# Score maxima of sliding-window attention in 9 products of 128 by 128 instead of 18 of 64 by 96, on one Trainium2 core

## The chip, the core and the metric

The kernel runs on one core of a Trainium2 chip. The metric is the device time of one launch in microseconds. Engines: PE multiplies matrices (PEld loads its weights), DVE and ACT work on vectors, POOL copies between SBUF tiles and issues the loads, SP issues the stores. Work of different engines is ordered by semaphores; each engine takes its own instructions in order.

## What is computed

Sliding-window causal attention over 8 batches of 8 heads, 576 positions, 64 channels, followed by a soft mixture of experts with 32 slots and 8 experts.

```python
scores = (q @ k.T) / 8                        # per batch and head, 576 x 576
mask = (i - j >= 0) & (i - j < 64)
scores = where(mask, scores, -1e9)
attn = exp(scores - scores.max(-1)); attn /= attn.sum(-1)
x = (attn @ v) laid out as 4608 x 512
logits = x @ phi                              # 4608 x 32
d = softmax of logits over the 4608 rows;  c = softmax over the 32 slots
slot = d.T @ x                                # 32 x 512, four slots for each expert
out = c @ (relu(slot[e] @ w1[e]) @ w2[e])     # w1: 8 x 512 x 1024, w2: 8 x 1024 x 512
```

All inputs are float32 in HBM and are turned into float16 by the DMAs that load them; the output, 9.4 MB, is float32.

## The kernel before

**Stages.** A loop of 32 stages works on pairs of heads, four pairs to a batch. The order on every engine is the order in which the program writes the work down; stage n runs several pairs at once, each at another step:

- `join(n+1)` (L108, POOL): two copies, of k and q, that bring a pair's rows together;
- `turn` (L259, PE) turns k and q of pair n; `keep_k` (L269) and `keep_q` (L266), on ACT, write `kT` and `qz`;
- `score_main(n-3)` (L320, L323, PE): for 8 blocks a product that adds mask and minus the row maximum (`lh` by `rt`), then the scores; `keep_main` (L328, ACT) takes their exponential into `pt`; `score_last` (L311, L312) and `keep_last` (L316, ACT) do the ninth block;
- `st_turn(n-5)`: `turn_x` (L363, PE) and `keep_x` (L370, DVE) turn the finished x;
- `st_mask` (L274, L275) and `st_max(n-1)` (L291, PE): masks and scores of pair n-1 once more, with queries on the partitions, into `mx`; `keep_max` (L296, DVE) takes the row maxima into `m`;
- `st_av(n-4)` (L340, PE) multiplies `pt` with the values; `st_norm` (L349, L350, DVE) divides;
- `st_shift(n-2)` (L300, PE) turns the maxima, `keep_shift` (L303, DVE) writes them into `rt`, where `score_main` finds them a stage later.

From stage 8 on each stage also has a quarter of the routing of a batch (`fi` in the code, here the letters A to D). A (`fi` 0): logits, copied by `keep_logits` (L384), and their maxima `nb`, `run` (L388, L389, DVE). B (`fi` 1): exponentials `dd` and `al` (L395, L396, ACT). C (`fi` 2): `turn_dispatch` (PE), `keep_dispatch` (L420, ACT, into `dT`), slot sums `si`, added up by `keep_slots` (L469, DVE). D (`fi` 3): an exponential (L431, ACT) and a transposition (L438, DVE).

**PSUM.** `kb`, `tx`, `qb` and `lg` or `si` share a ring of two banks; `sc`, `av` and `mx` have two banks each. `score_last` and `st_shift` use spare columns of `av`.

**Scores for the maxima before.** A block of 32 queries of two heads sees at most 96 keys, so that 18 products of 64 columns by 96 keys do, two to each block of 64 queries, one on the upper and one on the lower half of the partitions:

```python
for i in range(9):
    for t in range(2):
        o = 64 * i + 32 * t
        nc.tensor.matmul(mx[64 * t:64 * t + 64, i // 5, 96 * (i % 5):96 * (i % 5) + 96],
                         heads(p, o, 32), kT[:, o:o + 96], start=False, stop=True, ...)
```

**Loads.** POOL issues every load, between its copies: q and k of two pairs (`load_qk`), half a batch of values (`load_v`, then copied by `shift_v`), and weights (`load_w`), one transfer in every fourth stage and one in every stage from 25 on. The last six transfers are halves of the last three experts' `w2`.

**Tail.** After the loop the last pairs are finished, the slots go through the experts (`first` L800, `turned`, `second` L823), and `cps` (L861, ACT L865, DVE L867, store L869) writes the output in 19 stores, first the left half of the columns of two groups, then their right half, then two groups whole.

Of the kernel before, what the change touches and what calls it, by code (L numbers as in the profile page):

```python
# [20 lines left out]
def kernel(  # L21
# [114 lines left out]
    for t_, src in reversed(tuple(zip(firsts, (q, k)))):  # L136
# [9 lines left out]
    lh = const.tile([128, 9, 128], FP16, name="lh")  # L146
    nc.vector.memset(lh, 0.0)
    warm = lh[:, 0:4, :].rearrange("p i x -> p (i x)")
    NQ = 4
    qzs = [pqk.tile([128, 2 * S], FP16, name=f"qz{i}") for i in range(NQ)]  # L150
    kTs = [pqk.tile([128, 64 + S], FP16, name=f"kT{i}") for i in range(NQ)]
    sides[0] = (pil.tile([GP, RQ, 2, Dh], FP16, name="qi", tag="qi"),
                pil.tile([GP, RQ, 2, Dh], FP16, name="ki", tag="ki"))
    KR = 74
    nc.scalar.activation(lh[64:KR], ident_h[64:KR, 64:KR - 1].unsqueeze(2).broadcast_to([KR - 64, 9, 128]),
                         AF.Copy, scale=-1.0)
    nc.vector.memset(qzs[0], 0.0)
    nc.vector.memset(kTs[0][:, 0:64], 0.0)
    for t_, src, eng in zip(sides[0], firsts, (nc.scalar.copy, nc.vector.tensor_copy)):
# [3 lines left out]
    wb = ctr[0:32, 0:96]  # L163
    nc.gpsimd.memset(wb, 0.0)
    nc.gpsimd.affine_select(out=wb, in_=wb, compare_op=ALU.is_gt, fill=NEG,
                            base=0, pattern=[[1, 96]], channel_multiplier=-1)
    nc.gpsimd.affine_select(out=wb, in_=wb, compare_op=ALU.is_ge, fill=NEG,
                            base=64, pattern=[[-1, 96]], channel_multiplier=1)
    mb = ctr[0:64, 96:224]
# [6 lines left out]
    NR = 2  # L176
    sel = const.tile([128, 4, 32], FP16, name="sel")
    wm = const.tile([128, 5, 96], FP16, name="wm")
    for t in (0, 64):
        nc.vector.tensor_copy(out=sel[t:t + 32],  # L180
                              in_=ident_h[t:t + 32, t:t + 32].unsqueeze(1).broadcast_to([32, 4, 32]))
        nc.vector.tensor_copy(out=sel[t + 32:t + 64].rearrange("p (t l) x -> p t (l x)", t=2),
                              in_=ident_h[t + 32:t + 64, t + 32:t + 34].unsqueeze(2).broadcast_to([32, 2, 64]))
        nc.vector.memset(wm[t + 32:t + 64], 0.0)
        nc.vector.tensor_copy(out=wm[t:t + 32], in_=wb.unsqueeze(1).broadcast_to([32, 5, 96]))
    nc.vector.memset(wm[32:33, 0, 0:64], NEG)
    nc.vector.memset(wm[32:34, 0, 0:32], NEG)
    av = pav.tile([128, 2, 512], FP32, name="av", tag="av")
    mx = pmx.tile([128, 2, 512], FP32, name="mx", tag="mx")
    nc.vector.memset(mx[:, 1, 384:480], 0.0)  # L190
    ms = [const.tile([128, 33], FP16, name=f"m{i}") for i in range(2)]
    for t_ in ms:
        nc.vector.memset(t_[:, 10:33], 0.0)
    for t_, z_ in zip(kTs[1:], qzs[1:]):
        nc.vector.memset(t_[:, 0:64], 0.0)
        nc.vector.memset(z_, 0.0)
    nc.vector.memset(av[64:128, :, 260:325], 1.0)
    rts = [const.tile([128, 128], FP16, name=f"rt{i}") for i in range(NR)]
    for rt in rts:
        nc.vector.memset(rt, 0.0)  # L200
    for i in range(3):
        nc.vector.memset(vrs[i][:, :, 64], 1.0)
    for i in range(2):
        nc.vector.memset(vss[i][:, :, 64], 1.0)
        nc.vector.memset(vss[i][0:64, 0, 0:64], 0.0)
    lgs = pf.tile([128, 192], FP32, name="lgs")
    nc.vector.memset(lgs[0:96, 128:192], -3.0e38)
    dd = pf.tile([128, 256], FP16, name="dd")
    nc.vector.memset(dd[:, 192:256], 0.0)
    run = pmo.tile([128, 3], FP32, name="run")  # L210
    stat, nmax = run[:, 0:1], [run[:, 1:2], run[:, 2:3]]
    nc.vector.memset(nmax[1], 1.0e30)
    nc.vector.memset(stat, 0.0)
# [6 lines left out]
    def constants(part):  # L220
        if part == 2:
            nc.vector.tensor_copy(out=lh[0:64], in_=mb[:, :].unsqueeze(1).broadcast_to([64, 9, 128]))
            for rt in rts:
                nc.vector.tensor_copy(out=rt[64:KR, :], in_=ident_h[64:KR, KR - 1:KR].broadcast_to([KR - 64, 128]))
                nc.vector.tensor_copy(out=rt[0:64, :].rearrange("p (t l x) -> p t l x", t=2, l=2),
                                      in_=ident_h[0:64, 0:64].rearrange("p (t x) -> p t x", t=2)
                                      .unsqueeze(2).broadcast_to([64, 2, 2, 32]))
            nc.vector.scalar_tensor_tensor(out=lh[64:KR, 0, 0:64],  # L228
                                           in0=ident_h[64:KR, KR - 1:KR].broadcast_to([KR - 64, 64]),
                                           scalar=NEG, in1=lh[64:KR, 0, 0:64], op0=ALU.mult, op1=ALU.add)  # L230
# [41 lines left out]
    def st_mask():  # L272
        st = sel.rearrange("p a x -> p (a x)")
        nc.tensor.matmul(mx[:, 0, 0:480], st[0:64], wm[0:64, 0:5, :], start=True, stop=False, skip_group_check=True)  # L274
        nc.tensor.matmul(mx[:, 1, 0:384].rearrange("p (c e x) -> p c e x", e=3, x=32)[:, :, 0::2, :],  # L275
                         st[64:128], wm[64:128, 1:5, :].rearrange("p c (e x) -> p c e x", e=3)[:, :, 0::2, :],
                         start=True, stop=False, skip_group_check=True)

    def heads(p, o, w):
        a = qzs[p % NQ][:, 2 * o:2 * o + 2 * w]  # L280
        return a if w == 32 else a.rearrange("p (t l x) -> p l t x", t=2, l=2)

    def turned_max(p):
        return rts[p % NR][:, :].rearrange("p (t l x) -> p l t x", t=2, l=2)

    def st_max(p):
        kT = kTs[p % NQ]
        for i in range(9):
            for t in range(2):
                o = 64 * i + 32 * t  # L290
                nc.tensor.matmul(mx[64 * t:64 * t + 64, i // 5, 96 * (i % 5):96 * (i % 5) + 96],  # L291
                                 heads(p, o, 32), kT[:, o:o + 96], start=False, stop=True,
                                 skip_group_check=True)

    def keep_max(p):
        nc.vector.reduce_max(ms[p % 2][:, 0:10].rearrange("p (h c) -> p h c", h=2),  # L296
                             mx[:, :, 0:480].rearrange("p h (c x) -> p h c x", x=96), axis=AXX)
# [4 lines left out]
    def keep_shift(p, to, eng=nc.vector.tensor_copy):  # L302
        eng(out=rts[p % NR][64:73, :], in_=to[0:9])  # L303
# [14 lines left out]
    def score_main(p, sc, u0=0, u1=2, o=0):  # L318
        for i in range(4 * u0, 4 * u1):
            nc.tensor.matmul(sc[:, i // 4 - o, 128 * (i % 4):128 * (i % 4) + 128], lh[:, i, :], turned_max(p),  # L320
                             start=(i % 4 == 0), stop=False, skip_group_check=True)
        for i in range(4 * u0, 4 * u1):
            nc.tensor.matmul(sc[:, i // 4 - o, 128 * (i % 4):128 * (i % 4) + 128],  # L323
                             kTs[p % NQ][:, 64 * i:64 * i + 128], heads(p, 64 * i, 64),
# [210 lines left out]
    for n in range(NP):  # L535
        b, hp = divmod(n, HP)
        if n + 1 < NP:
# [4 lines left out]
        elif n == 1:  # L542
            load_v(0, (1,))
            load_qk(3)
        elif n % 2 == 0 and n // 2 + 3 < 2 * B:
# [3 lines left out]
        constants(n)  # L549
# [16 lines left out]
        if n >= 3:  # L566
# [4 lines left out]
            score_last(n - 3, av[:, 0, 328:456])  # L571
            keep_last(n - 3, av[:, 0, 328:456])
# [6 lines left out]
        qb = bank([128, 1024], FP16, "qb")  # L579
        if fi == 2:  # L580
            turn_dispatch(qb[:, 640:800])
        turn(sides[n][0], qb)
        if fi == 2:
            keep_dispatch(fb, qb[:, 640:800])
        keep_q(n, qb)
        if n >= 1:
            st_mask()
        if n >= 4:
            st_av(n - 4, av)
        if n == NP - 3:  # L590
            to_row(nmax[O % 2], av[0:1, 0, 352:480])
        elif n == NP - 2:
            to_rows(rO, av[:, 0, 340:341])
        if n >= 2:
            st_shift(n - 2, av[64:97, 1, 384:512])
            keep_shift(n - 2, av[64:97, 1, 384:512])
        if n == NP - 3:
            row_min(rO, av[0:1, 0, 352:480])
            nc.gpsimd.tensor_scalar(out=pO, in0=nmax[O % 2], scalar1=-1.0, scalar2=None, op0=ALU.mult)
        elif n == NP - 2:  # L600
            nc.scalar.activation(fO, av[:, 0, 340:341], AF.Exp, bias=pO)
        if 4 <= n < NP - 1:
# [11 lines left out]
        if n >= 1:  # L614
            keep_max(n - 1)
        if fi == 0:
            keep_logits(lg, nc.vector.tensor_copy)
# [28 lines left out]
    R, W, X, Y = NP - 4, NP - 3, NP - 2, NP - 1  # L646
    kb = bank([128, 512], FP32, "kb")
# [260 lines left out]
```

## Time and profile before

| | us |
|---|---|
| three runs | 194.35, 195.71, 192.37 (median 194.35) |
| the profiled execution, its own time | 192.44 |
| its span in the profile | 190.7 |
| busy: PE, DVE, ACT, POOL | 155.2, 139.8, 129.3, 129.8 |
| mean granted clock of PE | 0.889 |
| read from HBM, written | 61.93 MB, 9.44 MB |

Busy time is the union of an engine's instructions. A row of the timeline gives the start, the time taken, the engine, the line, the operation, the tiles written and read, and in brackets the idle time before and what ended it. DMA shares count 16 engines as one; packets in flight together count twice, so that a share may be above 1.

### The profile page before, as it was taken

How to read it: one execution, taken by the hardware profiler on the slowest of the kernel's cores; microseconds unless marked ns; L12 is line 12 of the kernel's file. 1: busy time of each engine (PE TensorE's matmuls, PEld its weight loads, DVE VectorE, ACT ScalarE, POOL GpSimd, SP SyncE). 2: the span in 40 equal slices, each digit the busy share in tenths (PEclk: the TensorE clock that was granted, in tenths of full speed). 3: DMA queues.
4: the chain of work that ended last, by engine and by line, in shares of the span. 5: the costliest groups of instructions: out<-in, count | busy, mean ns of one | idle time of the engine just before them, and what ended most of it. 6: DMA issues, size and time to landing. Idle time of an engine off the chain costs nothing.

```text
span 190.7 us, 6941 instructions
## 1 busy us (share of the span) xinstructions
PE 155.2 (81%) x2897; PEld 116.2 (61%) x2897; DVE 139.8 (73%) x322; ACT 129.3 (68%) x244; POOL 129.8 (68%) x254
## 2 busy tenths in 40 slices
PE   1858888988898898988989779997888999999400
PEld 0538777867687677776868657676666446564000
DVE  4786688888799979978879987887775754689500
ACT  5672787879778797887977888787664052668400
POOL 8989999976979879888897877965988440000000
PEclk9975699999999999999999999999999699555555
DMA  6999999999999999999999999999999999999996
GB/s 149 148 184 184 201 199 184 173 224 177 184 220 183 183 221 180 185 223 178 182 215 188 188 217 211 198 213 213 217 218 199 198 198 180 249 342 342 399 415 269
DMA packets 64447, 41.14 MB, mean 216 GB/s; under 512 B 38816, under 2 KB 61856, under 8 KB 62880
## 3 DMA queue, kind: packets, MB, share of 16 engines
q0 software_dynamic: 58320, 30.68, 118.1%
q1 hardware_dynamic: 6096, 10.03, 14.6%
q8 instruction: 22, 0.36, 0.7%
q14 instruction: 9, 0.07, 0.1%
HBM read 61.93 MB, written 9.44 MB: 374 GB/s over the span
## 4 chain that ended last, share of the span: by engine, by line
PE 38%; DVE 32%; ACT 11%; issue 10%; POOL 2%; DVEq 0%; ACTq 0%; POOLq 0%
DVE m L296 9%; DVE x_b L350 8%; PE cp L861 7%; PE av L340 6%; ACT qz L266 3%; PE sc L320 3%; PE hh L800 3%; PE sc L323 3%; DVE rt L303 2%; PE ops L823 2%; ACT pt L328 2%; DVE rc L349 2%; PE mx L291 2%; PE qb L259 2%; ACT pt L316 2%
## 5 line engine op out<-in xcount | busy, mean ns | idle before, releaser
L266 ACT ACTIVATE qz<-qb 64x576 f16<-64x576 f16 x64 | 41.2, 643 | 1.8 <-PE qb L259 1.2
L296 DVE TENSOR_REDUCE m<-mx 128x10 f16<-128x960 f32 x32 | 36.8, 1149 | 0.6 <-PE mx L291 0.6
L328 ACT ACTIVATE pt<-sc 128x1024 f16<-128x1024 f32 x29 | 29.6, 1022 | 9.4 <-PE sc L323 8.7
L269 ACT ACTIVATE kT<-kb 128x576 f16<-128x576 f16 x32 | 20.8, 650 | 13.6 <-PE kb L259 13.2
L350 DVE TENSOR_TENSOR x_b<-av,rc 128x640 f16<-128x640 f32 x31 | 25.6, 824 | 1.1
L259 PE MATMUL qb<-ident_h,qi 96*128 96x96 f16 x192 | 14.2, 212 | 8.9 <-DVE acc L469 3.5
L303 DVE CAST rt<-av 9x128 f16<-9x128 f32 x30 | 8.7, 289 | 16.5 <-PE av L300 15.7
L117 POOL DMA_DIRECT2D vr<-in_v_dram x16 | 20.0, 1249 | 0.0
L323 PE MATMUL sc<-qz,kT 128*128 128x128 f16 x232 | 18.6, 223 | 0.7 <-issue 0.7
L320 PE MATMUL sc<-rt,lh 128*128 128x128 f16 x232 | 18.6, 225 | 0.6 <-DVE rt L303 0.6
L291 PE MATMUL mx<-kT,qz 128*64 128x96 f16 x576 | 18.7, 211 | 0.0
L340 PEld LDWEIGHTS <-pt 128*64 128x64 f16 x576 | 12.7, 110 | 9.3 <-ACT pt L316 4.4
L259 PEld LDWEIGHTS <-qi 96*128 96x128 f16 x192 | 11.5, 101 | 10.6 <-issue 9.5
L323 PEld LDWEIGHTS <-kT 128*128 128x128 f16 x256 | 16.5, 100 | 0.9 <-issue 0.9
L108 POOL COPY qi<-qs 96x384 int32<-96x384 int32 x31 | 15.6, 503 | 1.8 <-DMA qs<-in_q_dram 0.9
L320 PEld LDWEIGHTS <-lh 128*128 128x128 f16 x256 | 16.2, 100 | 0.7 <-DVE lh L228 0.4
L108 POOL COPY ki<-ks 96x384 int32<-96x384 int32 x31 | 15.6, 503 | 1.1
L865 ACT ACTIVATE ob<-cp,rcs 128x256 f32<-128x256 f32 (+1 forms) x27 | 13.2, 546 | 3.9 <-PE cp L861 3.6
L291 PEld LDWEIGHTS <-qz 128*64 128x64 f16 x576 | 15.6, 113 | 0.5 <-issue 0.4
L259 PE MATMUL kb<-ident_h,ki 96*128 96x96 f16 x192 | 14.6, 216 | 1.1 <-DVE xt L370 0.6
L340 PE MATMUL av<-vr,pt 128*64 128x65 f16 x279 | 15.4, 197 | 0.0
L340 PE MATMUL av<-vs,pt 128*64 128x65 f16 x279 | 13.7, 198 | 1.8 <-ACT pt L316 1.8
(198 smaller groups left out, 367.8 us busy)
## 6 DMA issues: line engine op xcount, KB each, us to landing
w<-in_moe_w_dram POOLq DMA_DIRECT2D x12, 1024.0 KB, 15.2
vr<-in_v_dram POOLq DMA_DIRECT2D x16, 288.0 KB, 11.8
out_dram<-ob SPq DMA_DIRECT2D x6, 768.0 KB, 7.0
ks<-in_k_dram POOLq DMA_DIRECT2D x15, 288.0 KB, 9.5
qs<-in_q_dram POOLq DMA_DIRECT2D x15, 288.0 KB, 10.3
out_dram<-ob SPq DMA_DIRECT2D x11, 384.0 KB, 4.3
w<-in_moe_w_dram POOLq DMA_DIRECT2D x8, 512.0 KB, 13.8
xt<-in_k_dram SPq DMA_DIRECT2D x1, 288.0 KB, 3.1
```

Of the source, the lines that this page charges most:

```text
L108: nc.gpsimd.tensor_copy(out=d_, in_=s_.rearrange("p h r d -> p r h d"))
L117: nc.gpsimd.dma_start(out=vrs[b % 3][:, c0:c1, 0:64], in_=src[:, c0:c1, :])
L259: nc.tensor.transpose(tp[:, j, :], src[:, j].rearrange("p h d -> p (h d)"), ident_h[0:GP, 0:GP])
L266: nc.scalar.activation(dst[r, hl], src[r], AF.Copy, scale=scale)
L269: nc.scalar.activation(kTs[p % NQ][:, 64:64 + S].rearrange("p (g j) -> p g j", j=RQ), ps[:, 0:RQ * GP].rearrange("p (j g) -> p g j", j=RQ) ...
L291: nc.tensor.matmul(mx[64 * t:64 * t + 64, i // 5, 96 * (i % 5):96 * (i % 5) + 96], heads(p, o, 32), kT[:, o:o + 96], start=False, stop=Tru ...
L296: nc.vector.reduce_max(ms[p % 2][:, 0:10].rearrange("p (h c) -> p h c", h=2), mx[:, :, 0:480].rearrange("p h (c x) -> p h c x", x=96), axi ...
L320: nc.tensor.matmul(sc[:, i // 4 - o, 128 * (i % 4):128 * (i % 4) + 128], lh[:, i, :], turned_max(p), start=(i % 4 == 0), stop=False, skip_ ...
L323: nc.tensor.matmul(sc[:, i // 4 - o, 128 * (i % 4):128 * (i % 4) + 128], kTs[p % NQ][:, 64 * i:64 * i + 128], heads(p, 64 * i, 64), start= ...
L328: nc.scalar.activation(pts[p][:, 0:8, :, :], sc[:, :, :].rearrange("p u (c l x) -> p (u c) l x", l=2, x=64), AF.Exp)
L340: nc.tensor.matmul(av[r0:r0 + 64, hl, 65 * (i // 2):65 * (i // 2) + 65], pt[:, i, hl, :], values(b, h, i), start=True, stop=True, skip_gro ...
L350: nc.vector.tensor_tensor(out=x_b[:, :, 128 * hp:128 * hp + 128].rearrange("p c (l d) -> p l c d", l=2), in0=avv[:, :, :, 0:64], in1=rc[:, ...
```

## The change

The scores for the maxima are made for 64 queries of two heads at a time, with 128 columns by 128 keys. Eight such products fill the two banks of `mx`, the ninth (`st_max_last`, `keep_max_last`, tile `m8`) goes to the columns of `av` that `score_last` had. The masks are no longer `sel` and `wm`; `st_mask` multiplies what `score_main` uses too (`lh`, `rt`), and a copy `low` for the lower half of the partitions. One row of `lh` falls away.

```diff
 def st_mask():
-    nc.tensor.matmul(mx[:, 0, 0:480], st[0:64], wm[0:64, 0:5, :], ...)
-    nc.tensor.matmul(mx[:, 1, 0:384] ..., st[64:128], wm[64:128, 1:5, :] ..., ...)
+    for r, u, keys in ((slice(0, 64), 0, lh[0:64, 0:4, :]), (slice(64, 128), 1, low[64:128, 1, :] x4)):
+        nc.tensor.matmul(mx[:, u, :], (low[r, 0, :] if u else rts[0][r, :]), keys, start=True, ...)
 def st_max(p):
-    for i in range(9): for t in range(2):  # 64 columns by 96 keys
+    for i in range(8):
+        nc.tensor.matmul(mx[:, i // 4, 128 * (i % 4):128 * (i % 4) + 128], queries(p, i),
+                         kTs[p % NQ][:, 64 * i:64 * i + 128], start=False, ...)
+def st_max_last(p, to):
+    nc.tensor.matmul(to, rts[0][0:64, :], lh[0:64, 8, :], start=True, stop=False, ...)
+    nc.tensor.matmul(to, queries(p, 8), kTs[p % NQ][:, 512:640], start=False, stop=True, ...)
 def keep_max(p):
-    nc.vector.reduce_max(ms[..][:, 0:10], mx[:, :, 0:480] by 96, axis=AXX)
+    nc.vector.reduce_max(ms[..][:, 0:8], mx by 128, axis=AXX)
+def keep_max_last(p, to):
+    nc.vector.reduce_max(ms[p % 2][:, 8:9], to, axis=AXX)
```

In the stage the order becomes this (`qz` has its heads in runs of 64 and no longer of 32):

```diff
             score_main(n - 3, sc); keep_main(n - 3, sc)
-            score_last(n - 3, av[:, 0, 328:456]); keep_last(n - 3, av[:, 0, 328:456])
 ...
         turn(sides[n][0], qb)
         if fi == 2: keep_dispatch(...)
-        keep_q(n, qb)
-        st_mask()
+        score_last(n - 3, s8)                   # s8: spare columns of qb
+        late = fi in (0, 2)
+        if not late: keep_q(n, qb); keep_last(n - 3, s8)
+        st_max_last(n - 1, m8)                  # m8: spare columns of av
         st_av(n - 4, av)
         st_shift(n - 2, ...)
-        keep_shift(n - 2, ...)                  # DVE
+        keep_shift(n - 2, ..., nc.scalar.copy if fi in (0, 2) else nc.vector.tensor_copy)
+        if late: keep_q(n, qb); keep_last(n - 3, s8)
         st_norm(n - 4, av)
+        keep_max_last(n - 1, m8)
+        st_mask()
         st_max(n - 1)
 ...
-            keep_logits(lg, nc.vector.tensor_copy)
+            keep_logits(lg, nc.scalar.copy)
```

At the start, PE's first products read a cleared `qz` tile, without the wait for ACT's first write to `lh`; the constants are written in another order, several of them only at the ends of stages 2 and 3. `join(3)` moves from the head of stage 2 to the end of stage 1, ahead of that stage's `load_v` and `load_qk(3)`; `join(4)` moves from the head of stage 3 to the end of stage 2, ahead of `load_qk(4)`, `shift_v(0, 0)` and `load_w`, which move with it. In the tail the last pair's ninth product has a bank and a reduction of its own.

More of the change, by code (lines that the diff above doesn't have):

```diff
@@ L151 @@
     kTs = [pqk.tile([128, 64 + S], FP16, name=f"kT{i}") for i in range(NQ)]
+    warm = qzs[NQ - 1][:, 0:512]
+    nc.vector.memset(qzs[NQ - 1], 0.0)
+    lh = const.tile([128, 9, 128], FP16, name="lh")
+    nc.vector.memset(lh[64:128], 0.0)
+    KR = 73
+    nc.scalar.activation(lh[64:KR], ident_h[64:KR, 64:KR].unsqueeze(2).broadcast_to([KR - 64, 9, 128]),
+                         AF.Copy, scale=-1.0)
     sides[0] = (pil.tile([GP, RQ, 2, Dh], FP16, name="qi", tag="qi"),
                 pil.tile([GP, RQ, 2, Dh], FP16, name="ki", tag="ki"))
-    KR = 74
-    nc.scalar.activation(lh[64:KR], ident_h[64:KR, 64:KR - 1].unsqueeze(2).broadcast_to([KR - 64, 9, 128]),
-                         AF.Copy, scale=-1.0)
     nc.vector.memset(qzs[0], 0.0)
     nc.vector.memset(kTs[0][:, 0:64], 0.0)
+    NR = 2
+    rts = [const.tile([128, 128], FP16, name=f"rt{i}") for i in range(NR)]
+    by_head = lambda ap: ap.rearrange("p (l x) -> p l x", l=2)
+    for rt in rts:
+        nc.vector.memset(rt[64:128], 0.0)
+        nc.vector.tensor_copy(out=by_head(rt[0:64, :]), in_=ident_h[0:64, 0:64].unsqueeze(1).broadcast_to([64, 2, 64]))
+    low = const.tile([128, 2, 128], FP16, name="low")
+    nc.vector.tensor_copy(out=by_head(low[64:128, 0, :]),
+                          in_=ident_h[64:128, 64:128].unsqueeze(1).broadcast_to([64, 2, 64]))
     for t_, src, eng in zip(sides[0], firsts, (nc.scalar.copy, nc.vector.tensor_copy)):
@@ L174 @@
                             fill=NEG, base=0, pattern=[[-1, 64]], channel_multiplier=1)
[L176 to L185, printed above, removed]
@@ L197, with clear @@
[L197 to L205, printed above, removed]
+        nc.vector.memset(t_[:, 9:33], 0.0)
+    def clear(i):
+        nc.vector.memset(kTs[i][:, 0:64], 0.0)
+        if i < NQ - 1:
+            nc.vector.memset(qzs[i], 0.0)
@@ L206 @@
+    clear(1)
+    nc.vector.tensor_copy(out=lh[0:64], in_=mb.unsqueeze(1).broadcast_to([64, 9, 128]))
+    nc.vector.memset(lh[0:64, 0, 0:64], NEG)
+    nc.vector.tensor_copy(out=low[64:128, 1, :], in_=mb)
+    clear(2)
+    clear(3)
     lgs = pf.tile([128, 192], FP32, name="lgs")
-    nc.vector.memset(lgs[0:96, 128:192], -3.0e38)
     dd = pf.tile([128, 256], FP16, name="dd")
-    nc.vector.memset(dd[:, 192:256], 0.0)
     run = pmo.tile([128, 3], FP32, name="run")
     stat, nmax = run[:, 0:1], [run[:, 1:2], run[:, 2:3]]
-    nc.vector.memset(nmax[1], 1.0e30)
@@ L221, in constants @@
         if part == 2:
[L222 to L230, printed above, removed]
+            nc.vector.memset(av[64:128, :, 260:325], 1.0)
+            for i in range(3):
+                nc.vector.memset(vrs[i][:, :, 64], 1.0)
+            for i in range(2):
+                nc.vector.memset(vss[i][:, :, 64], 1.0)
+                nc.vector.memset(vss[i][0:64, 0, 0:64], 0.0)
+        elif part == 3:
+            nc.vector.memset(lgs[0:96, 128:192], -3.0e38)
+            nc.vector.memset(dd[:, 192:256], 0.0)
+            nc.vector.memset(nmax[1], 1.0e30)
+            nc.vector.memset(stat, 0.0)
         elif part == 4:
@@ L283, in turned_max @@
-    def turned_max(p):
-        return rts[p % NR][:, :].rearrange("p (t l x) -> p l t x", t=2, l=2)
-    def st_max(p):
[L287 to L293, printed above, removed]
+        for r, u, keys in ((slice(0, 64), 0, lh[0:64, 0:4, :]),
+                           (slice(64, 128), 1, low[64:128, 1, :].unsqueeze(1).broadcast_to([64, 4, 128]))):
+            nc.tensor.matmul(mx[:, u, :].rearrange("p (c y) -> p c y", c=4), (low[r, 0, :] if u else rts[0][r, :]), keys,
+                             start=True, stop=False, skip_group_check=True)
@@ L536 @@
         b, hp = divmod(n, HP)
-        if n + 1 < NP:
+        if n + 1 < NP and n not in (2, 3):
             join(n + 1)
@@ L542 @@
         elif n == 1:
-            load_v(0, (1,))
-            load_qk(3)
-        elif n % 2 == 0 and n // 2 + 3 < 2 * B:
+            pass
+        elif n % 2 == 0 and n > 2 and n // 2 + 3 < 2 * B:
             load_qk(n // 2 + 3)
@@ L579, with keep_both @@
         qb = bank([128, 1024], FP16, "qb")
+        s8 = qb.bitcast(FP32)[:, 384:512]
         if fi == 2:
-            turn_dispatch(qb[:, 640:800])
+            turn_dispatch(qb[:, 576:736])
         turn(sides[n][0], qb)
         if fi == 2:
-            keep_dispatch(fb, qb[:, 640:800])
-        keep_q(n, qb)
+            keep_dispatch(fb, qb[:, 576:736])
+        if n >= 3:
+            score_last(n - 3, s8)
+        late = fi in (0, 2)
+        def keep_both():
+            keep_q(n, qb)
+            if n >= 3:
+                keep_last(n - 3, s8)
+        if not late:
+            keep_both()
+        m8 = av[:, 0, 328:456]
         if n >= 1:
-            st_mask()
+            st_max_last(n - 1, m8)
         if n >= 4:
@@ L590 @@
         if n == NP - 3:
-            to_row(nmax[O % 2], av[0:1, 0, 352:480])
+            tr = bank([1, 128], FP32, "tr")
+            to_row(nmax[O % 2], tr)
         elif n == NP - 2:
-            to_rows(rO, av[:, 0, 340:341])
+            to_rows(rO, av[:, 1, 340:341])
         if n >= 2:
             st_shift(n - 2, av[64:97, 1, 384:512])
-            keep_shift(n - 2, av[64:97, 1, 384:512])
+            keep_shift(n - 2, av[64:97, 1, 384:512], nc.scalar.copy if fi in (0, 2) else nc.vector.tensor_copy)
+        if late:
+            keep_both()
         if n == NP - 3:
-            row_min(rO, av[0:1, 0, 352:480])
+            row_min(rO, tr)
             nc.gpsimd.tensor_scalar(out=pO, in0=nmax[O % 2], scalar1=-1.0, scalar2=None, op0=ALU.mult)
         elif n == NP - 2:
-            nc.scalar.activation(fO, av[:, 0, 340:341], AF.Exp, bias=pO)
+            nc.scalar.activation(fO, av[:, 1, 340:341], AF.Exp, bias=pO)
         if 4 <= n < NP - 1:
@@ L615 @@
             keep_max(n - 1)
+        if n == 1:
+            join(3)
+            load_v(0, (1,))
+            load_qk(3)
+        elif n == 2:
+            constants(2)
+            join(4)
+            load_qk(4)
+            shift_v(0, 0)
+            load_w(1)
+        elif n == 3:
+            constants(3)
         if fi == 0:
-            keep_logits(lg, nc.vector.tensor_copy)
+            keep_logits(lg, nc.scalar.copy)
             fr_max(fb)
@@ L646 @@
     R, W, X, Y = NP - 4, NP - 3, NP - 2, NP - 1
+    m8 = bank([128, 128], FP32, "m8")
+    st_max_last(Y, m8)
+    keep_max_last(Y, m8)
     kb = bank([128, 512], FP32, "kb")
```

56 lines of the change are left out of this document (17 added, 39 removed).

## The prediction

> **What bounds the kernel now.** I read the busy line and the DMA line of the page first, then windows over the end of the span, then the tiles of the last loads and of the stores.
>
> ```profile
> PE 155.2 (81%) x2897; PEld 116.2 (61%) x2897; DVE 139.8 (73%) x322; ACT 129.3 (68%) x244; POOL 129.8 (68%) x254
> DMA  6999999999999999999999999999999999999996
> ```
> ```profile
> 155.00:160.00 5.00, 4.81 (x85) 2.63 (x85) 1.18 (x2) 1.54 (x3) 0.16 (x1) 1.00 1.45 198
> 162.00:164.00 2.00, 2.00 (x11) 1.29 (x10) 2.00 (x6) 2.00 (x7) 0.00 (x0) 0.53 0.75 133
> 164.00:166.00 2.00, 1.98 (x27) 0.85 (x25) 1.07 (x3) 0.85 (x2) 0.00 (x0) 0.50 1.00 324
> 185.00:189.00 4.00, 0.00 (x0) 0.00 (x0) 0.00 (x0) 0.00 (x0) 0.00 (x0) 0.50 1.00 410
> 189.00:190.70 1.70, 0.00 (x0) 0.00 (x0) 0.00 (x0) 0.00 (x0) 0.00 (x0) 0.50 0.00 0
> ```
> ```profile
> L69 POOL DMA_DIRECT2D w<-in_moe_w_dram x11: 528/873/942, 113.6 to 146.1; - x11
> ...
> DMA to landing us min/median/max: 9.3/14.8/20.4
> ```
> ```profile
> L869 SPq DMA_DIRECT2D out_dram<-ob x19: 370/1032/1344, 161.8 to 181.0; - x19
> ...
> DMA to landing us min/median/max: 3.5/4.4/8.6
> ```
>
> No engine is busy throughout; the DMA line is, in every slice but the first and the last. In a windows row the last three numbers are clock, DMA share and GB/s. The weights issued last, at 146.1, take up to 20.4 us to land, so loads run until about 165 however early they were issued. The first store is issued at 161.8, the last at 181.0, and it lands up to 8.6 later: the stores queue behind each other until 189, when traffic stops and the kernel ends. Two things set the end: the load queue, empty at 165, and the moment from which stores keep the DMAs full. The engines' chain decides the second. It has little room: between 162 and 164 the DMA share is already 0.75, so a quarter of these 2 us, 0.5, is what a full queue would use better. I take 0.5 us of room (bounds 0.2 and 0.8, since the edges of that gap are not sharp). So a loop that ends earlier gains almost nothing, and one that ends later by T costs T - 0.5.
>
> The loop's pace is seen in two stages of a batch (B from 71.78, C from 75.56), and in the chain of waits:
>
> ```profile
> 71.78 0.43 PE L259 MATMUL kb<-ident_h,ki 96*128 96x96 f16 x6
> 72.24 0.65 ACT L269 ACTIVATE kT<-kb 128x576 f16<-128x576 f16 x1 [0.60 <-PE kb L259]
> 73.20 1.02 ACT L328 ACTIVATE pt<-sc 128x1024 f16<-128x1024 f32 x1 [0.31 <-PE sc L323]
> 74.71 0.46 ACT L395 ACTIVATE dd<-lgs,run 128x192 f16<-128x192 f32 x1 [0.32 <-DVE run L389]
> 75.35 1.28 ACT L266 ACTIVATE qz<-qb 64x576 f16<-64x576 f16 x2
> 75.56 0.43 PE L259 MATMUL kb<-ident_h,ki 96*128 96x96 f16 x6
> 76.66 0.65 ACT L269 ACTIVATE kT<-kb 128x576 f16<-128x576 f16 x1
> 77.21 1.02 ACT L328 ACTIVATE pt<-sc 128x1024 f16<-128x1024 f32 x1
> 78.11 0.28 ACT L316 ACTIVATE pt<-av 128x128 f16<-128x128 f32 x1
> 78.27 0.31 ACT L420 COPY dT<-qb 128x160 f16<-128x160 f16 x1
> 78.44 1.32 ACT L266 ACTIVATE qz<-qb 64x576 f16<-64x576 f16 x2
> 78.45 0.22 PE L340 MATMUL av<-vs,pt 128*64 128x65 f16 x1 [0.21 <-ACT pt L316]
> 79.07 0.29 DVE L303 CAST rt<-av 9x128 f16<-9x128 f32 x1 [0.21 <-PE av L300]
> 79.81 0.28 PEld L259 LDWEIGHTS <-ki 96*128 96x128 f16 x6 [0.42 <-POOL run L412]
> ```
> ```profile
> 63.78 0.82 DVE x_b L350
> ...
> 66.79 0.21 PE mx L274
> ...
> 67.53 0.39 PE mx L291 x18
> 67.92 0.36 PE kb L259 x6
> 68.28 0.45 PE sc L320 x8
> ...
> 79.64 0.82 DVE x_b L350
> ```
>
> A batch takes 15.86 us (79.64 - 63.78). From the start of B to that of D (79.81) ACT hardly rests; D and A take the other 7.83. D starts right after `qz` of C ends (78.44 + 1.32 = 79.76), since that frees the bank of `qb`.
>
> **The products.** Before, 18 products take 0.39 a stage; eight of 128 by 128 take 0.45 (row sc), the ninth and its mask 0.11 more. Both masks together took 0.21 for 480 columns, so 512 cost 0.22. PE gets 0.18 a stage more, not less: the 18 are half as wide and run in pairs.
>
> The Trainium skill, "TensorEngine Tiling (Array Packing)", section Tiling Modes, says that two tiles of 128 rows by 64 columns work independently; the trace agrees, 0.39 for 18. One after another at half the pair's 0.043 each rate they would take 0.78, and the change would save 0.22 a stage; by the rule it saves nothing.
>
> **The reductions.** Rows of groups:
>
> ```profile
> L296 DVE TENSOR_REDUCE m<-mx 128x10 f16<-128x960 f32 x32 | 36.8, 1149 | 0.6 <-PE mx L291 0.6
> L388 DVE TENSOR_REDUCE nb<-lgs 128x1 f32<-128x192 f32 x6 | 2.1, 353 | 0.2
> L494 DVE TENSOR_REDUCE vr<-av 1x32 f32<-1x128 f32 x1 | 0.3, 281 | 0.0
> ```
>
> From 192 to 960 elements the time rises by 1.04 ns each; 1024 cost 1.22, 128 between 0.281 and 0.353, 0.29 taken. DVE gets 0.36 a stage, and gives up `rt` (0.29) in A and C and `lgs` in A (two copies, 0.56 to the next). Over a batch 1.44 against 1.14: +0.3, hidden by DVE's idle time in C and A. ACT gets what DVE gives up.
>
> **The order, from B to D.** In the changed program the waits differ in three ways. (1) The ring's next `kb` after A and C waits for `keep_last`, which stands behind `keep_q`. (2) In A and C `keep_q` stands behind `keep_shift` on ACT, so behind PE's `st_av`. Behind them in turn are `kT` and all of the next stage. (3) `score_last` in C waits for `dT`, which reads the same bank. I add starts: B's `kb` at 0; `pt` 1.42 (73.20 - 71.78); no wait for `run` any more (DVE has no `lgs` to copy, so it is early); `dd` 0.90 after `pt` (as 78.11 after 77.21), 2.32; `qz` 0.64 later, 2.96; `qz` takes 1.28, then `keep_last`, 4.24; `kT` 0.15 later, 4.39; `pt` 0.55 later, 4.94; `dT` 0.90 later, 5.84, ending 6.15; 0.05 to PE; `score_last` 0.11 and `st_max_last` 0.11, `st_av` starts at 6.42; `rt` 0.62 later (79.07 - 78.45), 7.04; `qz` 0.16 later, 7.20, ending 8.52; `keep_last` 0.28 and 0.05 to PE: D's `kb` at 8.85. Before it was 8.03 (79.81 - 71.78). **+0.82.** Between 6.15 and 7.04 ACT waits for PE: the place of the loss. What the removed wait for `run` (0.32) and the earlier `kT` won is spent there.
>
> The Trainium skill, "PSUM — Partial Sum Buffer", section PSUM bank collisions, says to guard PSUM by bank and quadrant, not by address. The trace agrees: `av` at 78.45 starts 0.06 after `keep_last` ends (78.39), though they use different columns. Without that, `score_last` would come right after its turns and C would be some 0.5 shorter, the batch +0.3; by the rule it is not.
>
> **D and A.** In A `kb` to `st_av` is 0.26 + 0.91 + 0.28 + 0.35 + 0.22 = 2.02 by the same rows, `rt` 2.64, `qz` 2.80 to 4.09, release 4.42; before 3.86 (71.78 - 67.92). D was 7.83 - 3.86 = 3.97 on the mean; with `mx`'s mask and `av`'s wait out of PE's way it is bound by PE and by DVE's sum of slots, 3.2 to 3.5. Together 7.6 to 7.9: no change, 7.8 taken. A batch then takes 8.85 + 7.8 = 16.65, **+0.8** (bounds: +0.3 if (3) costs nothing, +1.2 if DVE's 0.3 and PE's 0.72 a batch show in part). Six batches, stages 8 to 31: **+4.8** (1.8 to 7.2).
>
> **Start to stage 8.**
>
> ```profile
> 15.50 0.67 POOL L96 DMA_DIRECT2D ks<-in_k_dram  x1
> ...
> 18.85 0.50 POOL L108 COPY ki<-ks 96x384 int32<-96x384 int32 x1
> ...
> 19.75 1.23 POOL L117 DMA_DIRECT2D vr<-in_v_dram  x1
> ...
> 21.71 0.52 POOL L108 COPY ki<-ks 96x384 int32<-96x384 int32 x1
> ```
> ```profile
> ks<-in_k_dram POOLq DMA_DIRECT2D x15, 288.0 KB, 9.5
> ```
> ```profile
> 35.92 0.43 PE L259 MATMUL kb<-ident_h,ki 96*128 96x96 f16 x6
> ```
>
> PE and DVE start sooner by some 2 us, but `join(4)` reads what is issued just before 10 us and lands 9.5 later, about 18.7: it ends at 19.25, as late as before (19.8) within 0.5. Then stand the loads, `shift_v` and `load_w` that it was moved past (18.85 - 15.50 = 3.35) and `load_v` with `phi` (21.71 - 19.75 = 1.96) before `join(5)`: 24.5, where it was at 21.71. The SP queue holds no load then. With POOL's 3.5 and 3.0 us for the next three stages, stage 8 begins at 35.2 instead of 35.92: **-0.7** (-2.2 if POOL is not the bound there, +0.5 if it stays behind). From 8 on POOL catches up, since a batch of 16 us has 2 us of idle POOL.
>
> **Tail.** One more reduction and bank: +0.2 (0 to 0.5).
>
> **Sum.** 4.8 - 0.7 + 0.2 = 4.3 later at the first store, minus 0.5 of room: 3.8. On the profiled execution's own time, 192.44, that is 196.2. It is the low end of three runs whose median is 194.35 (192.37 to 195.71), so I put the changed median at 194.35 + 3.8 = **198.1**, its own range 196.6 to 200.1. I also take it that loads still end at 165: the issue of weights slips by at most 4.3, and they wait 9.3 or more in the queue.
>
> **Rivals.**
> 1. *The loads hide it; not slower.* If D and A win back what C loses (D down to 3.1, POOL's lead in stages 4 to 8 the full 2.2), the loop ends 0.5 late at most, the stores still start behind the last weights, and the time stays at 194.35. It decides below T = 0.5. For it: PE's waits for `m` and `av` go; against it: ACT's 0.9 us wait in C is new. 194.4.
> 2. *ACT and PE meet in every stage.* If PE's 0.18 and the later `kT` show in A and D too, a batch costs +1.4: 8.4 - 0.7 + 0.2 - 0.5 = 7.4; 201.7. For it: PE holds 81% already; against: its waits fall in B and D.
> 3. *Half as many score-maximum products and the early start pay.* The whole queue of loads would have to move, by at most the 1 to 2 us that the start is under its later rate: 192.9.
>
> **Chances.** Forecast 0.54, rival 1 0.27, rival 2 0.14, rival 3 0.05. A measurement of this kernel tells about 2% (3.9 us) from no change: 198.24. Half of the forecast (0.27) and all of rival 2 lie above; below it by 2% lies under half of rival 3, with 0.02 for what I overlook. Faster 0.04, same 0.54, slower 0.42. The range, 193.2 to 201.2, takes in rival 1 with part of the runs' spread, and the nearer half of rival 2.
>
> **What would show it.** In the profile after: batches of 16.6 (starts of `x_b` in equal stages); ACT idle for 0.9 before `rt` in C, ended by PE; PE's first turn of B and D ended by ACT's `pt`; `mx` 0.45 for eight; `join(5)` near 24.5; loads landing until 165 and first store near 166, with a DMA share well under 0.75 between. It is wrong if batches stay at 15.9, if the first store comes by 162, or if the load queue runs dry inside the loop.

## The result, and the profile after

The changed kernel takes 204.1 us (median of six; 203.33 to 204.91) against a median of 195.03 for the kernel before in the same runs. Three of the six runs of the kernel before were in a slower state of the chip (195.71 to 196.34), so the ratio, 1.0575 (interval 1.0505 to 1.0646), is that of the means of the others, 204.17 and 193.07. Forecast were 198.1 and a range of 193.2 to 201.2, with a chance of 0.54 for no change beyond 2% and of 0.42 for slower; the forecast time moved the right way, but by too little. The profiled executions are 203.77 and 192.44, their spans 202.0 and 190.7.

The page of the changed kernel, busy line and DMA line; then the groups of the late weights and of the stores (issue times, and the time from issue to landing of each tile's transfers):

```profile
PE 165.8 (82%) x2641; PEld 122.3 (61%) x2641; DVE 138.7 (69%) x319; ACT 136.1 (67%) x268; POOL 128.9 (64%) x251
DMA  6999999999999999999999999999999999599995
```
```profile
L69 POOL DMA_DIRECT2D w<-in_moe_w_dram x11: 531/873/942, 120.6 to 156.7; - x11
...
L885 SPq DMA_DIRECT2D out_dram<-ob x19: 369/1000/1426, 173.1 to 191.8; - x19
```

PE has 256 matmuls fewer than before and is busy 10.6 us longer. The first store leaves at 173.1 instead of 161.8, 11.3 later, and the span is 11.3 longer: the whole loss is there before the first store.

| starts, us | before | after | later by |
|---|---|---|---|
| `kb` of stage 8 | 35.92 | 37.13 | 1.21 |
| `kb` of stage 28 | 115.81 | 123.94 | 8.13 |
| `kb` of stage 31 | 128.47 | 138.49 | 10.02 |
| last `x_b` | 142.14 | 153.52 | 11.38 |
| first store | 161.78 | 173.11 | 11.33 |

So 1.2 is lost before stage 8, 8.8 in the stages, 1.4 behind them. Two starts of `x_b` in equal stages of the changed kernel give a batch of 17.37, where it was 15.86:

```profile
66.97 0.82 DVE L336 TENSOR_TENSOR x_b<-av,rc 128x640 f16<-128x640 f32 x1
...
84.34 0.82 DVE L336 TENSOR_TENSOR x_b<-av,rc 128x640 f16<-128x640 f32 x1
```

What PE waits for, over three batches from `kb` of stage 16 to `kb` of stage 28 (columns: total, times, longest). Before, 67.85 to 115.81:

```profile
PE qb L259 <- DVE acc L469: 2.1, 3, 0.7
PE qb L259 <- DVE lgs L384: 1.8, 3, 0.6
PE mx L274 <- DVE m L296: 0.8, 3, 0.3
PE av L340 <- ACT pt L316: 0.7, 3, 0.3
PE sc L323 <- issue: 0.4, 1, 0.4
```

After, 71.82 to 123.94:

```profile
PE kb L248 <- ACT pt L302: 3.6, 6, 0.6
PE qb L297 <- ACT dT L406: 1.7, 3, 0.6
```

Before, 5.8 of 47.96 us are waits; after, 5.3 of 52.12. The waits have changed their names and hardly their sum. What grew is the rest: 42.2 us in three batches became 46.8, 1.55 more a batch, 0.39 a stage.

From `kb` to `kb`, in the batch that begins with stage 16, the stages take:

| stage | before | after |
|---|---|---|
| A | 3.93 | 4.69 |
| B | 3.78 | 3.42 |
| C | 4.25 | 5.79 |
| D | 3.90 | 3.47 |

The loss stands in A and C. B and D even got shorter, since PE no longer waits in them. Stage B, from its `qb` to the next `kb`, shows what PE's time consists of (most of the value products are left out). Before:

```profile
74.09 0.42 PE L259 MATMUL qb<-ident_h,qi 96*128 96x96 f16 x6 [0.60 <-DVE lgs L384]
74.44 0.37 PE L274 MATMUL mx<-wm,sel 64*128 64x480 f16 x1
74.74 0.22 PE L340 MATMUL av<-vs,pt 128*64 128x65 f16 x1
...
75.02 0.22 PE L300 MATMUL av<-ident_h,m 128*33 128x128 f16 x1
75.08 0.55 PE L291 MATMUL mx<-kT,qz 128*64 128x96 f16 x18
```

After:

```profile
77.93 0.42 PE L248 MATMUL qb<-ident_h,qi 96*128 96x96 f16 x6
78.19 0.22 PE L297 MATMUL qb<-rt,lh 128*128 128x128 f16 x1
78.25 0.22 PE L298 MATMUL qb<-qz,kT 128*128 128x128 f16 x1
78.40 0.23 PE L276 MATMUL av<-lh,rt 64*128 64x128 f16 x1
78.56 0.23 PE L277 MATMUL av<-kT,qz 128*128 128x128 f16 x1
78.72 0.22 PE L326 MATMUL av<-vs,pt 128*64 128x65 f16 x1
...
79.00 0.22 PE L286 MATMUL av<-ident_h,m 128*33 128x128 f16 x1
79.15 0.39 PE L264 MATMUL mx<-lh,rt 64*128 64x512 f16 x1
...
79.48 0.62 PE L272 MATMUL mx<-kT,qz 128*128 128x128 f16 x8
79.93 0.42 PE L248 MATMUL kb<-ident_h,ki 96*128 96x96 f16 x6
```

The starts are what to read, since a matmul's own 0.22 overlaps with the next. Two full matmuls of 128 columns start 0.06 apart (78.19, 78.25). Where the shape of the weights changes (64*128 is 64 rows, 128*64 is 64 columns) the next one starts 0.15 to 0.16 later: 0.10 more each time. The ninth mask has 64 rows between full products and so brings two such changes. The stage before has three of them (turns to masks, masks to values, maxima to the next turns), the changed one five (ahead of the ninth mask and behind it, ahead of the values, ahead of the masks and behind them).

### The profile page after: what moved, and what is told of

Its sections match the earlier page's. It is cut to its first block, busy times and chain, and to the rows that moved or that the text cites. A ratio compares the mean times of both kernels' runs of the same rounds, so it can differ in the third digit from the quotient of the medians.

```text
span 202.0 us, 6419 instructions
## 1 busy us (share of the span) xinstructions
PE 165.8 (82%) x2641; PEld 122.3 (61%) x2641; DVE 138.7 (69%) x319; ACT 136.1 (67%) x268; POOL 128.9 (64%) x251
## 4 chain that ended last, share of the span: by engine, by line
PE 47%; ACT 22%; DMA 7%; issue 6%; DVE 6%; POOL 6%; POOLq 0%; ACTq 0%; DVEq 0%
ACT qz L255 11%; DMA qs<-in_q_dram 7%; PE cp L877 6%; PE av L326 5%; PE sc L309 5%; PE sc L306 5%; PE kb L248 4%; PE mx L272 3%; ACT pt L314 2%; PE tx L349 2%; ACT pt L302 2%; PE qb L248 2%; PE ops L839 2%; PE av L277 2%; PE av L276 2%
## 5 line engine op out<-in xcount | busy, mean ns | idle before, releaser
L280 DVE TENSOR_REDUCE m<-mx 128x8 f16<-128x1024 f32 x32 | 38.9, 1216 | 2.4 <-PE mx L272 2.4
L258 ACT ACTIVATE kT<-kb 128x576 f16<-128x576 f16 x32 | 20.7, 648 | 11.3 <-PE kb L248 10.4
L272 PE MATMUL mx<-kT,qz 128*128 128x128 f16 x256 | 21.1, 229 | 0.0
L248 PEld LDWEIGHTS <-ki 96*128 96x128 f16 x192 | 11.3, 102 | 14.8 <-issue 8.7
L272 PEld LDWEIGHTS <-qz 128*128 128x128 f16 x256 | 15.3, 102 | 7.7 <-issue 7.7
L309 PE MATMUL sc<-qz,kT 128*128 128x128 f16 x232 | 18.1, 222 | 0.0
L289 DVE CAST rt<-av 9x128 f16<-9x128 f32 x18 | 5.2, 289 | 15.3 <-PE av L286 15.3
L326 PE MATMUL av<-vr,pt 128*64 128x65 f16 x279 | 15.5, 198 | 0.0
L335 DVE RECIPROCAL rc<-av 128x10 f32<-128x10 f32 x31 | 6.8, 220 | 12.5 <-ACT rt L289 7.7
```

What stands on the lines that cost most here:

```text
L248: nc.tensor.transpose(tp[:, j, :], src[:, j].rearrange("p h d -> p (h d)"), ident_h[0:GP, 0:GP])
L258: nc.scalar.activation(kTs[p % NQ][:, 64:64 + S].rearrange("p (g j) -> p g j", j=RQ), ps[:, 0:RQ * GP].rearrange("p (j g) -> p g j", j=RQ) ...
L272: nc.tensor.matmul(mx[:, i // 4, 128 * (i % 4):128 * (i % 4) + 128], queries(p, i), kTs[p % NQ][:, 64 * i:64 * i + 128], start=False, stop ...
L280: nc.vector.reduce_max(ms[p % 2][:, 0:8], mx[:, :, :].rearrange("p u (c y) -> p (u c) y", y=128), axis=AXX)
L326: nc.tensor.matmul(av[r0:r0 + 64, hl, 65 * (i // 2):65 * (i // 2) + 65], pt[:, i, hl, :], values(b, h, i), start=True, stop=True, skip_gro ...
```

## Experiments

The loss was taken apart by undoing one thing at a time in the changed kernel. Medians, each with the ratio to the kernel before, run beside it. The rows were measured at different times, so the ratios compare them better; differences below are of medians. The intervals of three rows overlap with that of the changed kernel (first stages in the old order, narrow products, PE kept busy): there the traces carry the reading.

| kernel | us | ratio, interval |
|---|---|---|
| changed | 204.1 | 1.0575, 1.0505 to 1.0646 |
| ninth mask with 128 rows | 199.56 | 1.0383, 1.0264 to 1.0502 |
| `keep_q`, `keep_last` early in A and C | 209.7 | 1.0863, 1.0766 to 1.096 |
| `score_last` ahead of the dispatch turns | 200.14 | 1.0386, 1.029 to 1.0482 |
| first stages in the old order | 201.39 | 1.0441, 1.0353 to 1.0528 |
| first, third and fourth together | 193.88 | 1.0058, 1.0019 to 1.0096 |
| early, and `keep_shift` on DVE | 200.15 | 1.0349, 1.0261 to 1.0438 |
| all five | 194.67 | 1.0052, 0.9998 to 1.0106 |
| 16 narrow products | 206.06 | 1.066, 1.0581 to 1.0739 |
| PE kept busy in stage 4 | 203.97 | 1.0617, 1.054 to 1.0694 |

### The ninth mask with 128 rows

```diff
+    one9 = const.tile([128, 128], FP16, name="one9")      # as rts[0] above row 64, zeros below
-        nc.tensor.matmul(to, rts[0][0:64, :], lh[0:64, 8, :], start=True, ...)
+        nc.tensor.matmul(to, one9, lh[:, 8, :], start=True, ...)
```

> The changed kernel with one edit: the ninth mask has all 128 rows (a constant with zeros below row 64) instead of 64. Its size on PE stays 128 columns. Theory (change of row or column tiling drains PE): in the changed kernel the matmul after each change of tiling starts 0.15 to 0.16 after the one before it, not 0.06, and the ninth mask makes two such changes a stage; without them B and D, where PE has no wait, go from 3.43 to 3.23, and a batch from 17.36 by 0.8 to 16.5; the time falls by about 5 us to 199. Rival (a lone pair of products is slow because it changes operands and bank, not because of the tiling): starts stay 0.15 apart, B and D stay at 3.43, time 204.

```profile
76.05 0.22 PE L300 MATMUL qb<-rt,lh 128*128 128x128 f16 x1
76.11 0.22 PE L301 MATMUL qb<-qz,kT 128*128 128x128 f16 x1
76.16 0.22 PE L279 MATMUL av<-lh,one 128*128 128x128 f16 x1
76.22 0.22 PE L280 MATMUL av<-kT,qz 128*128 128x128 f16 x1
76.37 0.22 PE L329 MATMUL av<-vs,pt 128*64 128x65 f16 x1
```

The same four products, same bank, same columns: the starts around the ninth mask are now 0.05 and 0.06 apart, and only the change to the values still costs 0.15. B and D go from 3.43 to 3.22, A from 4.69 to 4.53. C stays at 5.79: it begins 0.21 earlier, but PE waits in it for `dT`, which ACT starts 5.86 after B's `kb`, as late as without the edit (5.85); from B's `kb` to D's it is 9.00 instead of 9.21. A batch is 16.8 (forecast 16.5), stages 8 to 31 take 97.9 instead of 101.4, the time is 4.5 less. The shape of the weights, not the change of operands, is the price. The Trainium skill, "TensorEngine Tiling (Array Packing)", section Key Properties, says that a change of the tiling mode drains the engine; it gives no time. The traces agree with it: here a change cost 0.10 us each time.

### `keep_q` and `keep_last` ahead of the shift

```diff
-        late = fi in (0, 2)
+        late = False
```

> The changed kernel with one edit: keep_q and keep_last stand ahead of st_shift in stages A and C too, as they do in B and D. Theory (the next kb waits for keep_last, which stands behind a shift that PE does late): the waits of 0.65 and 0.55 us ahead of kb of B and D go, A from 4.69 to 4.04, C from 5.78 to 5.25, a batch from 17.36 to about 16.2, the time to about 197. Rival (PE's own work and the wait for dT set A and C, the order on ACT costs nothing): batch 17.3, time 204.

Slower by 5.6 instead of faster by 7: both theories missed. `keep_shift` of A and C is on ACT, and now stands behind `qz` and `keep_last` there. DVE's next operation on the bank waits for it, and with it everything behind, up to the sum `acc`, for which PE waits (a row of DVE, then one of PE):

```profile
69.68 0.22 DVE L335 RECIPROCAL rc<-av 128x10 f32<-128x10 f32 x1 [2.05 <-ACT rt L289]
```
```profile
72.80 0.41 PE L248 MATMUL qb<-ident_h,qi 96*128 96x96 f16 x6 [1.34 <-DVE acc L455]
```

With `keep_shift` on ACT the late order is the right one. The early order needs `keep_shift` off ACT as well.

### The same, with `keep_shift` on DVE

```diff
-        late = fi in (0, 2)
+        late = False
-            keep_shift(..., nc.scalar.copy if fi in (0, 2) else nc.vector.tensor_copy)
+            keep_shift(..., nc.vector.tensor_copy)
```

> The changed kernel with two edits: keep_q and keep_last ahead of st_shift in A and C, and keep_shift on DVE there too, so that it doesn't stand behind keep_q on ACT as in the kernel that was slower by 5.6. Theory (what cost there was the late copy of the shift, for which DVE's next operations waited; the early release of the ring's bank is a gain): the waits ahead of kb of B and D go, A 4.0, C 5.2, a batch 16.1 to 16.3, time 197. Rival (DVE, with 0.29 more in A and C, is what then binds): batch 16.8 or more, time 201 or more.

200.15, between the two, with a batch of 16.7 to 16.9. The waits ahead of `kb` are gone, A is 3.97, C 5.2 to 5.4; but D rises from 3.43 to 4.12. Part of the wait has moved to D, where PE waits for DVE's `acc` (DVE has two copies more in a batch):

```profile
85.32 0.42 PE L248 MATMUL qb<-ident_h,qi 96*128 96x96 f16 x6 [0.52 <-DVE acc L455]
```

### `score_last` ahead of the dispatch turns

```diff
+        if n >= 3 and fi == 2:
+            score_last(n - 3, s8)
         if fi == 2:
             turn_dispatch(qb[:, 576:736])
         turn(sides[n][0], qb)
...
-        if n >= 3:
+        if n >= 3 and fi != 2:
             score_last(n - 3, s8)
```

> The changed kernel with one edit: in stage C score_last is issued ahead of the two dispatch turns that share its bank, so it need not wait for dT's read. Theory (this wait is one link of the chain of C): PE's 0.57 us wait goes, C from 5.78 to 5.2, a batch to 16.8, the time to about 200.5. Rival (another wait takes its place, the value products or the shift being late anyway): C stays within 0.1 of 5.78, time 204.

C falls from 5.78 to 5.06, a batch to 16.65, the time by 4.0. In the waits of the same three batches only the first row is left:

```profile
PE kb L248 <- ACT pt L302: 3.6, 6, 0.7
```

### The first stages in the old order

```diff
-        if n + 1 < NP and n not in (2, 3):
+        if n + 1 < NP:
             join(n + 1)
...
-        if n == 1: join(3); load_v(0, (1,)); load_qk(3)
-        elif n == 2: constants(2); join(4); load_qk(4); shift_v(0, 0); load_w(1)
+        if n == 2: constants(2)
```
(`load_v`, `load_qk`, `load_w` and `shift_v` are back at the head of their stages.)

> The changed kernel with the order of joins, loads, shift_v and load_w of the first four stages put back as before, the constants left in their new order. Theory (join(5) late, PE idle for 2.4 and 1.0 us, and then at a granted clock of 0.5 for 5 us): join(5) ends by 22.7, no clock of 0.5 after 20 us, stage 8 starts near 35 instead of 37.1, the time falls by 1.5 to 2.5 us to 202. Rival (PE's clock drops for want of work whatever POOL does; the loads set the start): stage 8 stays at 37.

Stage 8 starts at 35.05 instead of 37.13 and the time falls by 2.7. In the changed kernel's windows the last three numbers are clock, DMA share and GB/s:

```profile
20.00:22.50 2.50, 0.65 (x22) 0.53 (x22) 0.32 (x4) 1.76 (x4) 2.42 (x5) 0.97 1.37 192
22.50:25.00 2.50, 1.53 (x11) 0.82 (x10) 2.38 (x5) 0.00 (x0) 2.46 (x4) 0.50 1.33 201
25.00:27.50 2.50, 2.47 (x25) 2.48 (x26) 1.49 (x10) 0.66 (x2) 2.50 (x4) 0.50 1.13 202
```

POOL works through, ACT soon has nothing to do, and PE, which waits for `shift_v` and then for `join(5)`, gets half its clock. `join(5)` began at 24.47; stage 5 then took 5.24, stages 6 and 7 took 3.43 each.

### PE kept busy in stage 4

```diff
+        if n == 4:
+            for _ in range(9):
+                nc.tensor.matmul(mx[:, 0, :], ident_h, warm[:, :], start=True, stop=True, ...)
         if n >= 4:
             st_av(n - 4, av)
```

> The changed kernel with one addition: nine idle products of 512 columns on PE in stage 4, in the 2.2 us in which PE waits for shift_v ahead of st_av; nothing of POOL's order is touched. Theory (half of the loss at the start is PE's granted clock, which falls to 0.5 between 22.5 and 27.5 because PE was idle): the clock stays at 1.00 there, stage 5 still begins at 25.0 but takes 3.5 to 3.9 and not 5.24, stage 8 begins near 35.6 instead of 37.13, the time falls by 1.5 to 202.6. Rival (POOL's late joins alone set these stages, the clock costs nothing beside them): stage 8 stays at 37, time 204.

```profile
22.50:25.00 2.50, 2.19 (x41) 1.33 (x39) 1.45 (x5) 0.40 (x2) 2.46 (x5) 1.00 1.32 209
25.00:27.50 2.50, 2.50 (x54) 2.09 (x50) 2.36 (x11) 2.11 (x3) 2.50 (x4) 1.00 1.21 202
...
140.00:144.00 4.00, 3.66 (x47) 2.60 (x47) 2.03 (x5) 1.65 (x4) 2.88 (x6) 0.68 1.02 213
```

The first half came as forecast: clock 1.00, stage 5 in 3.48, stage 8 at 35.74, with POOL's order untouched. The second did not: 203.97, no gain. Stage 31 still begins 1.4 earlier (137.09 against 138.49), but the last `x_b` comes at 153.37 against 153.52. Between 140 and 144 the granted clock is 0.68 in this profile and was 1.00. That fall does not account for the time, though: the other three runs, with a higher mean clock (0.912 to 0.915 against 0.893), took 203.71 to 204.39. So the clock explains the slow stage 5. That the old order kept its gain to the end and this one did not is seen; why is open.

### Three and five edits together

The first, third and fourth edits in one kernel:

> The changed kernel with three edits that were measured alone: the ninth mask with 128 rows (4.5 us won), score_last ahead of the dispatch turns in C (4.0), the first stages' joins and loads in the old order (2.7). Theory (three separate causes, in different stages and waits): the gains add, stage 8 at 34.4, a batch 15.9 (A 4.5, B 3.2, C 4.9, D 3.2), time 204.1 - 11.2 = 192.9, level with before. Rival (they share one chain, C's): C stays at 5.1, batch 16.1 or more, time 195 or more.

193.88: together the three win 10.2 of the 11.2 that they won singly by the medians; by the ratios they win 0.0517 of 0.0515, so they add. C is 5.06, as with the third alone, and not 4.9. The changed kernel is then within 1% of the one before (ratio 1.0058), its batch 16.06. With all five edits:

> The changed kernel with all five edits together. Theory of the prediction (loads keep the DMAs full and end at about 165, the stores queue behind): a batch of 15 or less, the last stage begins 7 us earlier than before, yet loads still land until 164 or later and the time stays at 192 to 194. Rival (the engines' chain sets the end, the first store follows the loop): the time falls by as much as the loop, to 187.

This one tests what sets the end. A batch takes 15.5 to 15.9, not 15 or less. The last stage begins at 124.16, 4.3 before that of the kernel before and not 7, the last `x_b` comes 3.4 earlier (138.76), and the last weights are issued at 142.1 instead of 146.1. The time is 194.67, not 187: the rival falls.

```profile
L69 POOL DMA_DIRECT2D w<-in_moe_w_dram x11: 528/873/942, 109.7 to 142.1; - x11
...
DMA to landing us min/median/max: 9.0/17.5/25.8
```
```profile
166.92 1.05 PE L837 MATMUL ops<-w,hT 128*32 128x256 f16 x16 [3.18 <-DMA w<-in_moe_w_dram]
```

The weights issued last, 4 us earlier than before, land at 166.9, and PE waits 3.2 us for them. The loads end no earlier for the shorter loop (before: 165). The first stores, issued at 160.3, now move beside the last loads; that this is what holds the loads up was not tried by itself. No version run here beats the kernel before.

### 16 narrow products

```diff
-            nc.tensor.matmul(mx[:, ...], queries(p, i), kTs[p % NQ][:, 64 * i:64 * i + 128], ...)
+            for l in range(2):
+                nc.tensor.matmul(mx[64 * l:64 * l + 64, ...], qzs[p % NQ][:, 128 * i + 64 * l:128 * i + 64 * l + 64], ...)
```

> The changed kernel with one edit: each of the 8 products of 128 columns in two of 64 columns (128 keys each), as the kernel before had them in pairs. Theory (two column tiles work at once, the number of products is not what costs): the group takes 0.45 as before the edit, batch 17.3, time 204. Rival (half as many instructions are a gain of the change): the group takes up to 0.9, B and D 3.9, time 208 or more.

```profile
71.13 0.39 PE L264 MATMUL mx<-lh,rt 64*128 64x512 f16 x1
...
71.45 0.64 PE L273 MATMUL mx<-kT,qz 128*64 128x128 f16 x16
72.02 0.43 PE L248 MATMUL kb<-ident_h,ki 96*128 96x96 f16 x6
```

The group takes 0.57 up to the next `kb`, against 0.45 (79.48 to 79.93 above): pairs run together, not one after another, but wide products are 0.12 better. From the mask to the first product it is 0.32 (71.13 to 71.45), as before the edit (0.33, 79.15 to 79.48): the change of shape ahead of the products stays, and a sixth one comes behind them, ahead of the turns. At 0.10 it is nearly all of the 0.12, so the pairs themselves are hardly slower. B and D are 3.53 to 3.59, not 3.9, and the time is 2.0 more, where the theory named none and the rival 4 or more: the wide products are a small gain of the change.

## Why the prediction was wrong, point by point

**What bounds the kernel: right.** The 11.38 us by which the last `x_b` is late arrive at the end but for at most 0.1 (11.3 in the span), where 0.5 of room was forecast. That a shorter loop gains nothing is borne out by the one kernel that has one, that with all five edits. One part was wrong: loads do not end at 165 however late they are issued. The last weights of the changed kernel leave at 156.7 (10.6 later; forecast was at most 4.3) and the last lands at 172.5. The queue was not full by then (DMA share 1.11 between 150 and 155, before 1.46), so what was issued late also ended late. Already in the loop the traffic falls to 115 GB/s between 96 and 101, where no slice of the page of before between 10 and 160 has less than 173. That the slower loop held its loads back there is a reading; it was not tried.

**The products and reductions: right singly.** Eight products 0.45, the reduction 1.216 (1.22 forecast), the ninth 0.28 (0.29).

**PE's time a stage: the step that failed.** Forecast were 0.18; measured 0.39. The missing 0.21 is what the ninth mask with 128 rows took away from B and D (3.43 to 3.22). The working priced each matmul by its columns alone, with no price for a change of shape. And it called this time covered, up to a part of it in the upper bound. In the changed kernel PE has no wait in B and D, so all of it shows there: the two stages are shorter than before, but by that much less. Rival 2, with PE's time showing in every stage, named 1.4 a batch (measured 1.5) and was given 0.14. It too priced PE at 0.18, so that its number is in part luck. Rivals 1 and 3 needed a loop that is hardly longer, or shorter; it is 8.8 longer.

**The order, from B to D: right until the ninth product.** Counted from B's `kb` at 76.51, `dd` was forecast at 2.32 and came at 2.32, `qz` 2.96 and 2.95, `keep_last` 4.24 and 4.25, `pt` 4.94 and 4.95, `dT` 5.84 and 5.85. Then `st_av`, forecast at 6.42, came at 6.74, since `score_last` and the ninth pair, four products, take 0.52 and not 0.22. `rt` comes at 7.29 (7.04) and D's `kb` at 9.21 (8.85). ACT's wait for PE in C is there, 1.12 where 0.9 was named:

```profile
82.36 0.31 ACT L406 COPY dT<-qb 128x160 f16<-128x160 f16 x1
83.80 0.26 ACT L289 CAST rt<-av 9x128 f16<-9x128 f32 x1 [1.12 <-PE av L286]
84.08 1.30 ACT L255 ACTIVATE qz<-qb 64x576 f16<-64x576 f16 x2
85.39 0.28 ACT L302 ACTIVATE pt<-qb 128x128 f16<-128x128 f32 x1
```

The wait for `dT` was priced at 0.5 a batch (0.8 with it, 0.3 without); with `score_last` ahead of the turns a batch is 0.7 shorter.

**D and A: 7.8 forecast, 8.12 measured** (A 4.69 for 4.42, D 3.43 for 3.2 to 3.5). Of A's 0.27, 0.16 go with the shape of the ninth mask (4.53 with 128 rows); the rest was not traced. (The working's 3.86 and 3.97 for A and D before are 3.93 and 3.90 from `kb` to `kb`; their sum is as it says.)

**Start to stage 8: wrong.** `join(5)` was forecast at 24.5 and began at 24.47. But the sum behind it counted POOL alone: that PE, idle meanwhile, would run the next stage at a clock of 0.50 was not in it. It comes out at +1.2 instead of -0.7, and with PE kept busy stage 8 begins 1.4 earlier (35.74): most of the difference is the clock.

**Tail: 1.4 instead of 0.2.** The kernel with three edits still has 14.82 us from the last `kb` to the last `x_b`, where before had 13.67. In the changed kernel 0.5 of it is lost ahead of the `qb` of stage 31, for which PE waits 1.53 for `acc` (before 1.05), and 0.7 from there to the first shift behind the loop (141.74 to 145.21; before 131.23 to 134.03), where the ninth products of the last two pairs now stand. Which of them it is was not tried.

**The sum.** 8.8 for 4.8, 1.2 for -0.7, 1.4 for 0.2, less 0.1: 11.3 for 3.8 on the profiled executions, and 11.1 between the two means that the ratio compares. Of the 7.5 that were missing, 4.0 are the loop's, and 3.4 of these go with the shape of the ninth mask (stages 8 to 31 in 97.9 instead of 101.4).

## What to carry to other kernels

Count what lies between the matmuls: each change between full, row-tiled and column-tiled weights cost 0.10 us here, and a small mask of 64 rows among full products pays it twice, more than its own columns. Before calling an engine's added work covered, ask in which stages that engine has a wait left; where waits only change their name, the added work is the loss. Where loads and stores keep the DMAs busy almost to the end, a shorter loop may win nothing: here the last `x_b` 3.4 us earlier brought none, and 11.4 later cost 11.3.

## What the hardware showed unexpectedly

PE's granted clock fell to 0.50 after a wait of 1.85 us (the two expectations on it say 2.4 and 2.2) with another of 1.0 behind it, and stayed there for over 6 us: it is 1.00 from 20.0 to 22.0, 0.85 in the next half us, 0.50 from 22.5 to 29.0 and 1.00 again from 29.5 on.

```profile
22.00 0.19 PE L326 MATMUL av<-vs,pt 128*64 128x65 f16 x1 [1.85 <-POOL vs L123]
...
25.03 0.42 PE L248 MATMUL kb<-ident_h,ki 96*128 96x96 f16 x3 [1.00 <-POOL ki L108]
```

The Trainium skill, "TensorE: Matmul & The Clock Gate", section Part 1, has the clock halved after an idle window of about 3.4 us. The trace agrees on the halving; the idle time that sufficed here was about half as long, in a program whose PE had been at 1.00 just before.
